# Attention, top-1 routing and two feed-forward layers on one core: the routing's row comparisons move between GpSimd, VectorE and ScalarE

## The chip, the cores and the metric

The kernel runs on one core of a Trainium2 chip. The metric is the device time of one execution in microseconds, the median of three runs. Engine names are those of the profile: PE is TensorE (PEld its weight loads), DVE is VectorE, ACT is ScalarE, POOL is GpSimd, SP is SyncE, which issues most DMAs.

## The reference, cut to what matters

```
x = attention(q, k, v)                  # 2 x 8 heads, 768 positions, window 128 and 4 sinks -> 1536 x 512
logits = x @ w_gate                     # 1536 tokens x 8 experts
for idx in argsort(-logits.flatten()):  # best (token, expert) pair first
    tok, e = idx // 8, idx % 8
    if assigned[tok] >= 0 or counts[e] >= 192: continue
    assigned[tok] = e; counts[e] += 1
for e in range(8):
    out[assigned == e] = relu(x[assigned == e] @ w1[e]) @ w2[e]     # 512 -> 1024 -> 512
g = prelu(out @ w_in, alpha)            # 512 -> 2048
return g @ w_out                        # 2048 -> 512
```

The loop over sorted pairs is a strict order of decisions, and the kernel has to give every token the same expert as that loop. It does so without a sort.

## The kernel before, in words

**Routing in stages.** Each stage closes one expert, the one that fills up first. Every living token has a best logit `m` among the experts still open and a one-hot row `oh` that names the expert. For a token t the kernel counts, per expert, how many living tokens have a better best logit (ties by index). The tokens whose count is below 192 for the expert that closes get it; its column is then struck out and the next stage begins. There are seven such stages (s = 0 to 6); the eighth expert takes what is left. Stages 0 and 1 work on 12 blocks of 128 tokens, stages 2 and 3 on 9, stages 4 to 6 on 6, because the living tokens are packed together between them by an indirect DMA each (`compact`).

**The counts.** `mrow` (128 x 1536, fp32) holds all best logits as one row, the same in each of the 128 partitions. For a block c1 of 128 tokens, whose own logits are a column `m[:, c1]`, the kernel makes a bf16 0/1 matrix `cm` (128 x 1536) of "row value is below own value", and PE multiplies it with `oh` of the block, 128 columns at a time (`count`, line 1042), and adds up over the blocks. A row of `cm` has three parts: the columns left of the block's own 128 (strictly below), the diagonal 128 columns (with the tie rule, through the constant triangle `tri`) and the columns to the right (below or equal).

There are two ways to make a block's `cm`:

- The direct way: one DVE `scalar_tensor_tensor` for the diagonal (line 991, `diag`) and one DVE `tensor_scalar` that compares fp32 to bf16 for each side (line 995, `side`).
- The way by differences (`via`): first the difference own minus row in bf16 (`minus`), in two instructions that together cover the row, on ACT (line 1000) or on POOL (line 1002), whichever the planner finds free first; then DVE compares the bf16 differences with zero (line 1010 for the sides, line 1006 for the diagonal).

Which blocks go by differences is set by `VIA`: in stage s those with `c1 * 7 % 12 < VIA[s]`. With VIA = (12, 6, 4, 2, 0, 0, 0) these are all blocks in stage 0, blocks 0, 2, 4, 7, 9, 11 in stage 1, 0, 2, 7 in stage 2, 0 and 7 in stage 3, and none later.

**Stage 0 in two groups.** Attention ends with the last token blocks. Stage 0 therefore starts on blocks 0 to 8 (columns 0 to 1151, group 0) while attention is still at blocks 9 to 11, and goes on with those (group 1) when their gate logits are there. In group 1 the old nine blocks get only the 384 new columns, by a direct comparison each (line 995), and the new three blocks get the whole row. The chain into group 1 is: transposes of x (PE, line 590), their high and low halves (ACT line 593, DVE line 595), gate (PE, line 619), logits (ACT, line 625), best logit (DVE, line 948), broadcast to `mrow` (PE line 976, ACT line 980).

After each stage the expert's tokens are named (`ohs`, line 1139, PE lines 1251 or 1273), their rows of x are gathered by an indirect DMA that POOL issues (line 1292), transposed on PE (line 1305), and the expert's two products follow (lines 1387 to 1394; experts 0 and 1 in plain fp32, line 1394, with their relu on ACT at line 1426). After two experts each, one chunk of 384 tokens runs through the last two layers (lines 1462 and 1483). Weights and activations of the later products are split into a high and a low half: the high half by ACT (line 1339), the low half by POOL or DVE (`lows`, line 1330). Line 807 is a step of unpacking w_in and w_out on POOL or DVE.

**What sets the order.** Each engine runs its instructions in the order in which a planner (`Plan.run`) emitted them. The planner is a list scheduler with an estimated time per task and engine. A task that names several engines goes to the first of them unless another would finish more than `bias` earlier (0.85 us by default; `EVEN` = 0.0 for the differences). So another estimate changes not only where a task goes, but the order of everything behind it. `cm` is a ring of 3 buffers (11 in stage 0): a buffer is written anew when PE has done the counts of its last user.

Of the kernel before, what the change touches and what calls it, by code (L numbers as in the profile page):

```python
# [211 lines left out]
AF = mybir.ActivationFunctionType  # L212
OP = mybir.AluOpType
# [24 lines left out]
def dve(n):  # L238
    return n / 960 + 0.065
# [491 lines left out]
def act_sb(n):  # L731
    return n / 1200 + 0.093
# [106 lines left out]
class Routed:  # L839
# [9 lines left out]
    BY_ROW = 2  # L849
    BY_DMA = (2, 3, 4, 5, 6)  # L850
    PLAIN, PLAIN2 = (0, 1), (0, 1)
    VIA = (12, 6, 4, 2, 0, 0, 0)

    def __init__(self, tc, nc, plan, ctx, logits, l_blocks, cd, md, xd, x_blocks, ident):
        self.tc, self.nc, self.plan, self.xd, self.x_blocks = tc, nc, plan, xd, x_blocks
# [71 lines left out]
    def closing(self, s, st, groups, r_bank, hold=(), fetched=False):  # L927

        nc, task, seq, ident, mrow, tri = self.nc, self.plan.task, self.seq, self.ident, self.mrow, self.tri  # L930
# [12 lines left out]
        for a, b in groups:  # L943
            n = b - a
# [11 lines left out]
            if fetched:  # L956
# [4 lines left out]
                     r=[m.part(a)], w=[ps], after=hold)  # L961
# [23 lines left out]
            for a1, b1 in done:  # L985
                for c1 in range(a1, b1):
                    cm, cut = self.r_cm.new(), []
                    at = c1 * 128

                    def diag(c1=c1, cm=cm, at=at):  # L990
                        nc.vector.scalar_tensor_tensor(cm.tile[:, at:at + 128], mrow[:, at:at + 128], m.tile[:, c1:c1 + 1],  # L991
                                                       tri, OP.subtract, OP.is_lt)

                    def side(x, y, op, c1=c1, cm=cm):
                        nc.vector.tensor_scalar(cm.tile[:, x:y], mrow[:, x:y], m.tile[:, c1:c1 + 1], None, op)  # L995

                    def minus(e, x, y, c1=c1, cm=cm):
                        to, rows_, own = cm.tile[:, x:y], mrow[:, x:y], m.tile[:, c1:c1 + 1]
                        if e == "ACT":
                            nc.scalar.activation(to, rows_, AF.Identity, scale=-1.0, bias=own)  # L1000
                        else:
                            nc.gpsimd.tensor_scalar(to, rows_, -1.0, own, OP.mult, OP.add)

                    def diag_d(cm=cm, at=at):
                        d = cm.tile[:, at:at + 128]
                        nc.vector.tensor_tensor(d, d, self.trih, OP.is_gt)

                    def side_d(x, y, op, cm=cm):
                        d = cm.tile[:, x:y]
                        nc.vector.tensor_scalar(d, d, 0.0, None, OP.is_gt if op is OP.is_lt else OP.is_ge)  # L1010

                    lo = 0 if a1 == a else a
                    via = a1 == a and (c1 * 7 % 12) < self.VIA[s]
                    rr = [m.part(a1), *(rows if a1 == a else fresh)]
                    if a1 == a:
                        sides = ((0, at, at + 128, None), (1, 0, at, OP.is_lt), (2, at + 128, b * 128, OP.is_le))
                    else:
                        sides = ((2, a * 128, b * 128, OP.is_le),)
                    if via:
                        for x, y, kk in ((0, at + 128, (0, 1)), (at + 128, b * 128, (2,))):  # L1020
                            if y > x:
                                n = y - x
                                seq.append(task({"ACT": act_sb(n), "POOL": n * 1.0e-3 + 0.02},
                                                lambda e, x=x, y=y, f=minus: f(e, x, y), r=rr, bias=self.EVEN,
                                                w=[cm.part(k) for k in kk if k != 1 or at]))
                    for k, x, y, op in sides:
                        if y == x:
                            continue
                        if op is None:
                            us, fn = (0.135, diag_d) if via else (0.265, diag)  # L1030
                        elif via:
                            us, fn = dve((y - x) / 4), lambda x=x, y=y, op=op, f=side_d: f(x, y, op)
                        else:
                            us, fn = dve((y - x) / 2) + 0.065, lambda x=x, y=y, op=op, f=side: f(x, y, op)
                        cut.append(cm.part(k))
                        seq.append(task({"DVE": us}, fn, r=() if via else rr, w=cut[-1:]))
                    counted.append(cnt.part(len(counted)))

                    def count(c1=c1, cm=cm, lo=lo, b=b):
                        begun.append(c1)  # L1040
                        for c in range(lo, b):
                            nc.tensor.matmul(v()[:, c], lhsT=cm.tile[:, c * 128:(c + 1) * 128], rhs=oh.tile[:, c1],  # L1042
                                             start=(len(begun) == 1 and c == lo),
                                             stop=(len(begun) == len(counted) and c == b - 1), skip_group_check=True)

                    task({"PE": 0.026 * (b - lo)}, count, r=[oh.part(a1), *cut], w=counted[-1:],
                         after=hold)
# [564 lines left out]
```

## Time and profile before

| what | value |
|---|---|
| time, median of 3 runs (lowest, highest) | 680.67 us (679.73, 681.04) |
| the profiled execution: its own time | 686.22 us |
| its span, first to last instruction | 684.5 us |
| PE, PEld busy | 598.6 us, 511.1 us |
| DVE, POOL, ACT busy | 486.9 us, 405.4 us, 393.0 us |

The stretches that the text speaks of, in microseconds from the start of the span: attention 0 to 117, stage 0 from 104 to 131 (group 0 to 118, group 1 from 118), stage 1 from 133 to 170 beside expert 0 (PE 146 to 178), the gather of expert 1's tokens to 184, expert 1 to 213, stages 2 and 3 from 208 to 305 beside the first chunk, stages 4, 5 and 6 around 390, 415 and 495 to 525. A busy time includes the time in which an instruction, already begun, is held up. A row of the timeline gives start, duration, engine, line, operation, tiles and shapes, the number of merged instructions, and in brackets the idle time before it with what ended it.

### The profile page before, as it was taken

To read this page: it belongs to the slowest core of one execution; us is meant where nothing else is said; L and a number is where in the kernel's file an instruction comes from. 1 tells how busy PE (TensorE), PEld (TensorE's weight loads), DVE (VectorE), ACT (ScalarE), POOL (GpSimd) and SP (SyncE) were. 2 spreads that over 40 slices of the span, in tenths; PEclk is the share of its full clock that TensorE was granted. 3 is DMA by queue.
4 is the path that set the end of the run, shared out by engine and by line. 5 is a ranking of instruction groups with operands and counts; after the bars stand their busy time and mean duration, and the time that the engine had idled before them with its cause. 6 is when DMAs were issued, how large, how long until landed. Compare 5 with 4: busy or idle time off the path is not lost.

```text
span 684.5 us, 12142 instructions
## 1 busy us (share of the span) xinstructions
PE 598.6 (87%) x4248; PEld 511.1 (75%) x4249; DVE 486.9 (71%) x1165; ACT 393.0 (57%) x835; POOL 405.4 (59%) x445
## 2 busy tenths in 40 slices
PE   5699996688688878789999989998998999899996
PEld 3467775467587766668889868697997888889994
DVE  4779998879656989882897587578766556874330
ACT  5668886364355755434776434377653447665552
POOL 4657735254734657446777655676675657766663
PEclk9589997569899889899999999999999999999999
DMA  7856343326877426003650021256000326500001
GB/s 208 257 109 141 94 94 109 124 95 233 284 264 236 124 62 220 24 0 107 218 155 5 24 93 47 93 173 209 28 1 0 116 63 197 190 30 1 0 1 46
DMA packets 41221, 76.57 MB, mean 112 GB/s; under 512 B 16324, under 2 KB 23016, under 8 KB 41064
## 3 DMA queue, kind: packets, MB, share of 16 engines
q1 hardware_dynamic: 38376, 68.87, 33.2%
q0 software_dynamic: 2784, 6.93, 3.0%
q8 instruction: 33, 0.54, 0.3%
q14 instruction: 28, 0.23, 0.1%
HBM read 66.75 MB, written 6.42 MB: 107 GB/s over the span
## 4 chain that ended last, share of the span: by engine, by line
PE 33%; DVE 11%; ACT 4%; DMA 3%; issue 2%; POOL 1%; POOLq 0%; ACTq 0%; DVEq 0%
PE o L1483 13%; PE h L1462 13%; PE h L1387 4%; DVE h L1379 3%; ACT spl L1339 2%; DVE spl L1330 2%; PE h L1389 2%; DVE cm L995 2%; DVE jt L1375 1%; DMA xg<-xd,sidx 1%; DMA raw<-w 1%; PE r L1305 1%; DVE x L1330 1%; DVE cm L991 1%; ACT jt L1374 1%
## 5 line engine op out<-in xcount | busy, mean ns | idle before, releaser
L1330 POOL TENSOR_TENSOR spl<-w,spl 128x512 fp32r<-128x512 f32 x107 | 143.7, 1345 | 91.0 <-ACT spl L1339 85.6
L1483 PE MATMUL o<-spl,gt 128*128 128x512 f32 x576 | 155.5, 414 | 4.7 <-DVE gt L1330 2.8
L1462 PE MATMUL h<-x,spl 128*128 128x384 f32 x768 | 150.3, 345 | 1.2 <-DVE x L1330 0.9
L1462 PEld LDWEIGHTS h<-x,spl 128*128 128x128 f32 x768 | 138.2, 193 | 7.7 <-DVE x L1330 2.6
L1483 PEld LDWEIGHTS o<-spl,gt 128*128 128x128 f32 x576 | 109.2, 196 | 26.7 <-DVE gt L1330 3.3
L1339 ACT CAST spl<-w 128x512 fp32r<-128x512 f32 x126 | 77.5, 616 | 30.7 <-PE o L1483 25.9
L1330 POOL TENSOR_TENSOR spl<-raw,spl 128x512 fp32r<-128x512 f32 x53 | 71.6, 1355 | 36.1 <-ACT spl L1339 26.1
L1466 ACT ACTIVATE t<-h,slope 128x384 f32<-128x384 f32 x64 | 37.1, 580 | 76.2 <-PE h L1462 76.2
L1468 DVE SCALAR_TENSOR_TENSOR v<-h,way,t 128x384 f32<-128x384 f32 x64 | 39.2, 613 | 55.7 <-ACT t L1466 55.7
L1339 ACT CAST spl<-raw 128x512 fp32r<-128x512 f32 x93 | 56.1, 620 | 19.6 <-PE o L1483 11.9
L1387 PE MATMUL h<-xT,spl 128*128 128x384 f32 x192 | 56.7, 363 | 9.4 <-DVE jt L1375 9.4
L1330 DVE TENSOR_TENSOR spl<-raw,spl 128x512 fp32r<-128x512 f32 x43 | 42.7, 994 | 25.5 <-ACT spl L1339 25.2
L1387 PE MATMUL h<-h,spl 128*128 128x384 f32 x192 | 55.9, 360 | 1.6 <-DVE jt L1375 1.4
L1470 ACT CAST gt<-v 128x384 fp32r<-128x384 f32 x64 | 32.9, 513 | 35.8 <-DVE v L1468 34.3
L1330 DVE TENSOR_TENSOR gt<-v,gt 128x384 fp32r<-128x384 f32 x39 | 38.2, 981 | 20.3 <-ACT gt L1470 20.3
L480 ACT ACTIVATE P<-sm,mn 128x260 f32<-128x260 f32 (+1 forms) x96 | 43.3, 490 | 10.4 <-DVE mn L469 9.6
L1389 PE MATMUL h<-xT,spl 128*128 128x192 f32 x192 | 48.0, 250 | 0.0
L1389 PE MATMUL h<-h,spl 128*128 128x192 f32 x192 | 48.0, 250 | 0.0
L1042 PEld LDWEIGHTS <-cm 128*128 128x128 bf16 x558 | 20.5, 100 | 35.0 <-DVE cm L995 24.4
L995 DVE TENSOR_SCALAR cm<-mrow,m 128x384 bf16<-128x384 f32 (+8 forms) x75 | 44.0, 624 | 1.1 <-ACT mrow L980 1.1
L1387 PEld LDWEIGHTS h<-xT,spl 128*128 128x128 f32 x192 | 36.0, 188 | 11.4 <-DVE jt L1375 11.2
L469 DVE CUSTOM_DVE_ANT_0 sm<-s,mask 128x260 f32<-128x260 f32 (+1 forms) x96 | 35.3, 398 | 10.9 <-PE s L459 10.8
(223 smaller groups left out, 1271.6 us busy)
## 6 DMA issues: line engine op xcount, KB each, us to landing
raw<-w SPq DMA_DIRECT2D x64, 512.0 KB, 3.9
r<-w_in SPq DMA_DIRECT2D x16, 512.0 KB, 4.2
r<-w_out SPq DMA_DIRECT2D x16, 512.0 KB, 4.7
vraw<-v SPq DMA_DIRECT2D x4, 768.0 KB, 10.4
xd<-x SPq DMA_DIRECT2D x12, 256.0 KB, 2.2
k<-kT SPq DMA_DIRECT2D x11, 260.0 KB, 5.6
q<-qT SPq DMA_DIRECT2D x11, 256.0 KB, 2.7
mrow<-md SPq DMA_DIRECT2D x2, 576.0 KB, 5.3
```

Source lines behind the costliest of these rows:

```text
L469: task({"DVE": dve(n)}, lambda: nc.vector.tensor_tensor_reduce(out=sm.tile[:, :n], in0=s.tile[:, :n], in1=mask[:, :n], scale=-0.125, scala ...
L480: task({"ACT": act(n) + 0.137}, lambda h=h, sm=sm, mn=mn: nc.scalar.activation(P[t].tile[:, h, :n], sm.tile[:, :n], AF.Exp, bias=mn.tile, ...
L995: nc.vector.tensor_scalar(cm.tile[:, x:y], mrow[:, x:y], m.tile[:, c1:c1 + 1], None, op)
L1330: eng.tensor_tensor(*aps(), OP.subtract)
L1339: (nc.scalar.copy if e == "ACT" else nc.vector.tensor_copy)(b.tile[:, 0], get())
L1387: nc.tensor.matmul(ps.tile[:, 0:2 * CAP], lhsT=w[:, 0, k], rhs=x.rearrange("p a t -> p (a t)"), start=first and k == 0, stop=False, skip_g ...
L1389: nc.tensor.matmul(ps.tile[:, CAP:2 * CAP], lhsT=w[:, 1, k], rhs=x[:, 0], start=False, stop=last and k == len(xs) - 1, skip_group_check=True)
L1462: nc.tensor.matmul(ps.tile[:, 0:CH], lhsT=w[:, i, k], rhs=x[:, j], start=(k == n == 0), stop=(k == KD - 1 and n == 2))
L1466: task({"ACT": act(CH)}, lambda: nc.scalar.activation(t.tile, ps.tile[:, 0:CH], AF.Copy, scale=slope), r=[ps, weights.way_res], w=[t])
L1468: task({"DVE": dve(CH) + 0.065}, lambda: nc.vector.scalar_tensor_tensor(v.tile, ps.tile[:, 0:CH], way, t.tile, OP.mult, OP.max), r=[ps, t, ...
L1470: task({"ACT": act_sb(CH)}, lambda: nc.scalar.copy(gt.tile[:, 0], v.tile), r=[v], w=[gt.part(0)])
L1483: nc.tensor.matmul(ops[t].tile, lhsT=gt.tile[:, i, sl], rhs=wo.tile[:, j], start=(f == n == 0), stop=(f == FB - 1 and n == 2))
```

## The change: what it does

```diff
-    VIA = (12, 6, 4, 2, 0, 0, 0)
+    VIA = (8, 6, 4, 2, 0, 0, 0)
+    SHORT = 768
...
-                    def side(x, y, op, c1=c1, cm=cm):
-                        nc.vector.tensor_scalar(cm.tile[:, x:y], mrow[:, x:y], m.tile[:, c1:c1 + 1], None, op)
-
-                    def minus(e, x, y, c1=c1, cm=cm):
-                        to, rows_, own = cm.tile[:, x:y], mrow[:, x:y], m.tile[:, c1:c1 + 1]
-                        if e == "ACT":
-                            nc.scalar.activation(to, rows_, AF.Identity, scale=-1.0, bias=own)
-                        else:
-                            nc.gpsimd.tensor_scalar(to, rows_, -1.0, own, OP.mult, OP.add)
+                    def side(e, x, y, op, c1=c1, cm=cm):
+                        (nc.gpsimd if e == "POOL" else nc.vector).tensor_scalar(cm.tile[:, x:y], mrow[:, x:y], m.tile[:, c1:c1 + 1], None, op)
+
+                    def minus(x, y, c1=c1, cm=cm):
+                        nc.scalar.activation(cm.tile[:, x:y], mrow[:, x:y], AF.Identity, scale=-1.0, bias=m.tile[:, c1:c1 + 1])
...
-                                seq.append(task({"ACT": act_sb(n), "POOL": n * 1.0e-3 + 0.02},
-                                                lambda e, x=x, y=y, f=minus: f(e, x, y), r=rr, bias=self.EVEN,
+                                seq.append(task({"ACT": act_sb(n) + 0.1}, lambda x=x, y=y, f=minus: f(x, y), r=rr,
                                                 w=[cm.part(k) for k in kk if k != 1 or at]))
...
+                        us = {}
                         if op is None:
-                            us, fn = (0.135, diag_d) if via else (0.265, diag)
+                            us["DVE"], fn = (0.135, diag_d) if via else (0.265, diag)
                         elif via:
-                            us, fn = dve((y - x) / 4), lambda x=x, y=y, op=op, f=side_d: f(x, y, op)
+                            us["DVE"], fn = dve((y - x) / 4), lambda x=x, y=y, op=op, f=side_d: f(x, y, op)
                         else:
-                            us, fn = dve((y - x) / 2) + 0.065, lambda x=x, y=y, op=op, f=side: f(x, y, op)
+                            us["DVE"], fn = dve((y - x) / 2) + 0.165, lambda e, x=x, y=y, op=op, f=side: f(e, x, y, op)
+                            if y - x <= self.SHORT or not s:
+                                us["POOL"] = (y - x) * 1.1e-3 + 0.15
                         cut.append(cm.part(k))
-                        seq.append(task({"DVE": us}, fn, r=() if via else rr, w=cut[-1:]))
+                        seq.append(task(us, fn, r=() if via else rr, w=cut[-1:], bias=self.EVEN if s == 0 else None))
```

Differences are formed by ACT alone; POOL forms none. The comparison of a side (line 995) may run on POOL as well as on DVE: in stage 0 for any width and wherever the planner expects the earlier end, in later stages for sides of up to 768 columns and only where POOL would end more than 0.85 us earlier. In stage 0 only the blocks with `c1 * 7 % 12 < 8` go by differences, which leaves blocks 3, 5 and 8 of group 0 and block 10 of group 1 to the direct way. The planner's estimate for a difference on ACT and for a direct comparison on DVE rises by 0.1 us each. What is computed stays the same.

## Rows read from the trace of the kernel before

**Rows 1.** The page: the line of the span and the busy times with their shares and instructions.

```profile
span 684.5 us, 12142 instructions
PE 598.6 (87%) x4248; PEld 511.1 (75%) x4249; DVE 486.9 (71%) x1165; ACT 393.0 (57%) x835; POOL 405.4 (59%) x445
```

**Rows 2.** Busy times by stretch: the stretch, its length, then busy time and instructions of PE, PEld, DVE, ACT and POOL, the granted clock of TensorE, the DMA share and GB/s. Group 0 and group 1 of stage 0, stage 1, the gather of expert 1, stages 2 and 3.

```profile
105.80:118.10 12.30, 7.22 (x143) 5.78 (x139) 11.63 (x37) 7.83 (x16) 8.31 (x10) 0.72 0.38 129
119.80:126.30 6.50, 3.11 (x51) 2.23 (x51) 6.31 (x17) 4.29 (x6) 2.22 (x2) 0.50 0.01 1
135.00:162.00 27.00, 22.86 (x219) 18.90 (x218) 22.37 (x48) 15.04 (x25) 13.61 (x11) 0.74 0.40 136
162.00:186.00 24.00, 17.38 (x124) 14.88 (x122) 18.87 (x53) 9.66 (x19) 14.76 (x20) 0.94 0.87 303
213.00:305.00 92.00, 76.20 (x459) 62.32 (x458) 83.16 (x158) 49.32 (x90) 53.94 (x43) 0.85 0.33 104
```

**Rows 3.** The waits of PE: whom it waited for, microseconds in total, times, longest. The first line is of the whole span; the others are what falls into 128 to 162, 215 to 262, 262 to 305, 385 to 402 and 490 to 526.

```profile
PE r L1042 <- DVE cm L995: 15.7, 17, 2.9
...
PE r L1042 <- DVE cm L995: 3.9, 4, 2.7
...
PE r L1042 <- DVE cm L995: 2.5, 3, 2.0
...
PE r L1042 <- DVE cm L995: 4.6, 4, 2.9
...
PE r L1042 <- DVE cm L995: 2.4, 3, 1.3
...
PE r L1042 <- DVE cm L995: 2.3, 3, 1.6
```

**Rows 4.** The timeline of group 0 of stage 0 and of the gate that opens group 1, on DVE, ACT and POOL.

```profile
106.79 7.83 POOL L1002 TENSOR_SCALAR cm<-mrow,m 128x896 bf16<-128x896 f32 x9 [0.44 <-ACT mrow L980]
112.35 1.05 DVE L1006 TENSOR_TENSOR cm<-cm,trih 128x128 bf16<-128x128 bf16 x1
112.79 0.69 ACT L593 ACTIVATE xT<-pt,scv 128x512 f16<-128x512 f32 x1 [0.25 <-PE pt L590]
113.33 1.46 DVE L1010 TENSOR_SCALAR cm<-cm 128x384 bf16<-128x384 bf16 x2
115.62 0.74 DVE L595 SCALAR_TENSOR_TENSOR xT<-pt,scv,xT 128x512 f16<-128x512 f32 x1
116.88 0.27 ACT L625 ACTIVATE L<-pv,scv 128x8 f32<-128x8 f32 x1 [3.12 <-PE pv L619]
116.99 0.21 DVE L1006 TENSOR_TENSOR cm<-cm,trih 128x128 bf16<-128x128 bf16 x1
117.53 0.21 DVE L1006 TENSOR_TENSOR cm<-cm,trih 128x128 bf16<-128x128 bf16 x1
118.00 0.16 DVE L948 TENSOR_REDUCE m<-L 128x3 f32<-128x24 f32 x1
```

**Rows 5.** The timeline of group 1 of stage 0, on POOL and DVE; the row at 120.22 holds two of the nine comparisons of the row at 119.89.

```profile
119.95 2.22 POOL L1002 TENSOR_SCALAR cm<-mrow,m 128x256 bf16<-128x256 f32 x2 [5.33 <-ACT mrow L980]
119.89 4.46 DVE L995 TENSOR_SCALAR cm<-mrow,m 128x384 bf16<-128x384 f32 x9 [1.09 <-ACT mrow L980]
120.22 2.16 DVE L995 TENSOR_SCALAR cm<-mrow,m 128x384 bf16<-128x384 f32 x2
122.30 0.40 DVE L995 TENSOR_SCALAR cm<-mrow,m 128x384 bf16<-128x384 f32 x1
124.27 0.21 DVE L1006 TENSOR_TENSOR cm<-cm,trih 128x128 bf16<-128x128 bf16 x1
125.69 0.51 DVE L1010 TENSOR_SCALAR cm<-cm 128x1408 bf16<-128x1408 bf16 x1
```

**Rows 6.** Single prices: the first three lines are of the timeline on POOL and DVE; the others are groups of instructions by shape, with busy time and the mean of one in ns.

```profile
138.58 0.38 POOL L1002 TENSOR_SCALAR cm<-mrow,m 128x128 bf16<-128x128 f32 x1
138.94 1.43 POOL L1002 TENSOR_SCALAR cm<-mrow,m 128x1408 bf16<-128x1408 f32 x1
...
395.03 0.34 DVE L991 SCALAR_TENSOR_TENSOR cm<-mrow,m,tri 128x128 bf16<-128x128 f32 x1
...
L1330 POOL TENSOR_TENSOR gt<-v,gt 128x384 fp32r<-128x384 f32 x25 | 28.0, 1120 | 20.6 <-ACT gt L1470 20.6
...
L995 DVE TENSOR_SCALAR cm<-mrow,m 128x1280 bf16<-128x1280 f32 x2 | 1.7, 873 | 0.0
...
L1000 ACT ACTIVATE cm<-mrow,m 128x1024 bf16<-128x1024 f32 x5 | 5.6, 1144 | 0.0
L1000 ACT ACTIVATE cm<-mrow,m 128x128 bf16<-128x128 f32 x5 | 2.0, 401 | 1.2 <-DMA mrow<-md 1.2
```

**Rows 7.** The timeline of stage 1 and of the gather behind it, on DVE, POOL and PE.

```profile
138.99 2.58 DVE L1006 TENSOR_TENSOR cm<-cm,trih 128x128 bf16<-128x128 bf16 x1 [1.47 <-POOL cm L1002]
140.34 1.15 POOL L807 TENSOR_TENSOR w<-w,sg 128x512 f32<-128x512 f32 x1
143.16 2.44 POOL L1002 TENSOR_SCALAR cm<-mrow,m 128x896 bf16<-128x896 f32 x1 [1.67 <-PE r L1042]
181.29 0.24 PE L1305 MATMUL r<-ident,xg 64*128 64x64 f32 x1 [3.00 <-DMA xg<-xd,sidx]
183.91 2.58 PE L1305 MATMUL r<-ident,xg 128*128 128x128 f32 x7 [2.38 <-DMA xg<-xd,sidx]
```

## The prediction, made before the changed kernel ran

> **What bounds the kernel now.** I read the busy times first [rows 1]: PE is busy for 598.6 of 684.5 us and the change touches none of its products, so what it can move is PE's idle time and whatever feeds PE. The stretches come second [rows 2]: PE works 7.2 of 12.3 us in group 0 and 3.1 of 6.5 us in group 1 of stage 0, at a granted clock of 0.72 and 0.50, while DVE is busy for 11.63 and 6.31 us of the same stretches. Routing there is a serial piece ahead of everything else, and DVE sets its length. Later PE is fuller and waits in places; its waits [rows 3] put 15.7 us down to DVE's direct comparisons (line 995): 3.9 us in stage 1, 2.5 and 4.6 us in stages 2 and 3, 2.4 us in stage 4, 2.3 us in stage 6. The timelines come last, because they show why DVE is slow there. In group 0 POOL forms nine differences without a break, 7.83 us, and in that time a DVE instruction of 0.21 us takes 1.05 us and two that follow take 1.46 us [rows 4]. In group 1 two comparisons take 2.16 us, beside POOL's 2.22 us, where one takes 0.40 us once POOL is done [rows 5]. In stage 1 one of 0.21 us takes 2.58 us and ends as POOL falls idle [rows 7]. So POOL and DVE hold each other up on these instructions, and the reader should see "DVE busy" there as partly waiting.
>
> **Stage 0, group 0.** Before, POOL has ten differences (6,272 columns, 8.31 us busy [rows 2]) and ACT seven (4,096 columns), counted one by one in the two timelines; together they are nine rows of 1,152. After, six blocks remain on ACT alone: 6,912 columns in 12 instructions. A difference costs 0.295 us plus 0.83 ns a column (from 1,144 ns for 1,024 and 401 ns for 128 [rows 6]); consecutive ones overlap by about 0.1 us, which is my estimate from the gap between their sum and ACT's busy time. That adds 2,816 x 0.83 ns = 2.3 us and five instructions of 0.2 us, 3.3 us in all, to an ACT that is idle for 12.30 - 7.83 = 4.5 us of this stretch [rows 2]. It fits, with 1.2 us to spare.
> On DVE an unhindered block by differences takes 0.54 us (116.99 to 117.53 [rows 4]); nine would take 4.9 us. Blocks 3, 5 and 8 now need a diagonal each (0.34 us as recorded [rows 6], 0.27 us less the 0.07 us by which such rows overlap: 0.40 us recorded, 0.33 us from start to start [rows 5]) and five sides (384, 640, 640, 384, 1,024 columns) that mostly go to an idle POOL. No row shows a comparison on POOL. From below I price it as POOL's difference, 0.27 us plus 0.82 ns a column (0.38 us for 128, 1.43 us for 1,408 [rows 6]), so 0.59 us for 384; from above as POOL's subtraction of two inputs, 1.12 us for 384 [rows 6]. I take the lower, because both are one-input instructions of the same shape on the same tiles. The five sides are then 3.9 us instead of 8.3 us of POOL, ending near 111 rather than 114.6, and DVE is free of POOL when the last gate comes.
> What that gives on the path: the low half for the gate (line 595) starts at 115.62 though its high half was ready at 113.48 (112.79 + 0.69), 2.1 us late, and the best logit (line 948) at 118.00 though the logits were ready at 117.15, 0.85 us late [rows 4]. Both go away at best: 3.0 us. ACT, now nearly full, may put one difference of up to 1.14 us ahead of line 593 and again ahead of line 625. So between -3.0 and -0.7 us; if ACT's queue runs over, up to +1.2 us. I take -1.4 us.
>
> **Stage 0, group 1.** Nine 384-column comparisons cost 0.33 us each from start to start when nothing holds them (122.30 to 124.27 for six [rows 5]), and POOL will take about four, since it is planned at 0.57 us (384 x 1.1 ns + 0.15) and DVE at 0.43 us, so that POOL ends earlier whenever DVE has one in hand. Block 10 goes direct: diagonal 0.27 us, 0.80 us for 1,280 columns (873 ns recorded [rows 6], less the overlap) and 0.19 us for 128. Blocks 9 and 11 keep 0.64 us each (124.27 to 124.91, and 0.65 us to 126.20). If POOL and DVE exclude each other the sum is 4 x 0.59 + 5 x 0.33 + 1.26 + 1.29 = 6.6 us against 6.31 us now; if they ran side by side it would be 4.2 us; if POOL also gets the 1,280 columns, 7.1 us; at the upper price 8.7 us. The rows show holding up, so I take +0.3 us, between -2.1 and +2.4. Stage 0 together: -1.1 us.
> [...]
> [...]
>
> **Stage 1.** POOL's five differences, one of them 2.44 us long for 896 columns [rows 7], move to ACT, which is busy for 15.04 of 27 us [rows 2]. With them goes most of the 2.37 us that DVE lost at 138.99, the rest of which is line 807's 1.15 us [rows 7], and the PE wait of 2.7 us behind it [rows 3]. PE's counts stand between expert 0's products, so a faster `cm` brings them forward only where the planner puts them forward. What the end of stage 1 sets is the gather of expert 1: PE waits 3.00 and 2.38 us for it [rows 7], 5.4 us, the most that can be had. Against it: the same five, 3,712 columns, cost ACT 3,712 x 0.83 ns + 5 x 0.295 us = 4.6 us, ahead of the relu of expert 0. Between -5.4 and +1.5 us; I take -1.5 us.
>
> **Stages 2 to 6.** Few differences leave POOL here: four in stages 2 and 3 by its timeline, none later. Sides of up to 768 columns may go to POOL where DVE is over 0.85 us behind. The four waits after 213 add up to 11.8 us [rows 3], the outer end of a gain. But POOL also makes the low halves that PE waits for, and every compare there holds DVE's diagonal. Between -4 and +2 us; I take -0.6 us.
>
> Sum: -1.4 + 0.3 - 1.5 - 0.6 = -3.2 us. The profiled execution took 686.22 us (span 684.5 us and 1.7 us around it), 5.55 us over the median of 680.67 us; a difference of this kind carries over as it is: 683.0 us for such an execution, 677.5 us for the median.
>
> **Rivals.**
> (1) The compares share out but the time doesn't fall. DVE and POOL take turns, the planner gives POOL little beyond stage 0 because of its bias (then the change does less than it says), and ACT's fuller queue eats what group 0 gains: 680.4 us. For it: the held-up rows. Against it: POOL's turns in group 0 halve in any case.
> (2) Slower: ACT becomes the bound. All differences pass through one queue. If the last one of group 0 ends after 117.2, where the logits are ready now, group 1 starts later by up to one wide difference, 1.14 us; in stage 1 two differences of 1,280 or 1,536 columns (about 1.4 us each) ahead of a relu leave PE without a free bank, since there are three. 1.1 + 2 x 1.4 - 0.9 (what DVE still gains) = +3.0 us: 683.7 us. For it: 1.2 us of slack. Against it: ACT is idle for 12 of 27 us in stage 1.
> (3) Slower: a compare on POOL costs like its two-input work, 1.12 us for 384 columns. Group 1 grows by 2.4 us and group 0 gains nothing (3,072 columns keep POOL as long as now), stage 1 gains half: 2.4 - 0.75 = +1.7 us, 682.4 us.
> (4) Much faster: stage 1 ends 4 us earlier so that the gather's wait nearly goes, and half of the 11.8 us of later waits melts through POOL: -1.1 - 4 - 3 = -8 us, 672.5 us.
>
> **How the numbers follow.** Forecast 0.50 (own range 674 to 679.5), (1) 0.21, (2) 0.13, (3) 0.06, (4) 0.10. About 0.2%, 1.4 us, is what a measurement tells from no change: faster takes the forecast without its edge, 0.47, and (4), 0.57; same takes (1) and that edge, 0.24; slower takes (2) and (3), 0.19. The range, 671 to 684 us, takes in the other cases except the far half of (4) and of (2), and covers that any new estimate reorders all instructions behind it.
>
> **What would show it.** Right: in group 0 DVE rows of line 1006 fall to 0.21 us after about 111; line 948 starts near 116.5 instead of 118.00; in group 1 POOL holds about four 384-column compares near 0.6 us, and DVE rows beside them stretch; the wait for expert 1's gather is below 5.4 us. Wrong: POOL's compare of 384 columns near 1 us; ACT without gaps up to line 625; PE waits for `cm` from POOL; or line 995 nearly all on DVE after stage 0.

## The result, and the profile after

The changed kernel took 687.88 us (median of 4 runs, 686.28 to 688.18), the kernel before beside it 680.86 us (679.73 to 681.93): ratio 1.0111 [1.0074, 1.0148], slower by 7.0 us. The forecast was 677.5 us, range 671 to 684: the sign was wrong and the time lies outside the range. The profiled execution of the changed kernel took 687.92 us. The profiled execution of the kernel before was a slow one: up to its first best logits, which start at 104.20 us and in the other traces at 99 to 102, its granted clock was 0.89 against 1.00 in the changed kernel, and behind them the two differ by 0.03 at most, so stages are compared below from that instruction on.

The page of the changed kernel, span and busy times, beside [rows 1]:

```profile
span 686.2 us, 12140 instructions
PE 599.8 (87%) x4248; PEld 513.6 (75%) x4249; DVE 484.6 (71%) x1150; ACT 401.1 (58%) x849; POOL 420.1 (61%) x439
```

PE's work is the same to 1.2 us. POOL is busy for 14.7 us more, with six instructions fewer. Most of that is the exchange itself: its 21 differences took 21.0 us before, its 19 comparisons take 34.0 us now.

The waits of PE over the whole span (whom for, microseconds in total, times, longest), beside the first of [rows 3]:

```profile
PE r L1041 <- DVE cm L996: 15.7, 11, 6.0
PE s L1041 <- POOL cm L996: 7.4, 5, 3.0
PE r L1041 <- POOL cm L996: 3.7, 2, 2.2
```

Line 996 is now the comparison of a side (995 before), 999 ACT's difference, 1041 the count. 11.1 us of waits for POOL's comparisons are new: 7.4 us in stage 0 (tile `s`), 3.7 us in stage 1 (`r`). The wait for DVE's comparisons has the same sum as before, 15.7 us, but not in the same places. In stage 1 the 3.9 us of before are gone; behind stage 1 the wait has grown from 11.8 us [rows 3] to the whole 15.7 us. What falls into 214 to 305, 385 to 440 and 490 to 540 (stages 2 and 3, 4, 6):

```profile
PE r L1041 <- DVE cm L996: 11.8, 5, 6.0
...
PE r L1041 <- DVE cm L996: 2.4, 3, 1.3
...
PE r L1041 <- DVE cm L996: 1.5, 3, 0.8
```

Stretches of the changed kernel, columns as in [rows 2]: group 0, group 1, stage 1.

```profile
101.60:111.20 9.60, 6.30 (x135) 5.43 (x131) 8.88 (x29) 9.29 (x19) 7.81 (x4) 0.69 0.42 140
112.60:122.40 9.80, 2.52 (x58) 2.04 (x59) 5.99 (x15) 4.93 (x7) 8.79 (x5) 0.50 0.00 1
131.00:162.00 31.00, 24.72 (x226) 20.98 (x225) 22.25 (x47) 18.89 (x31) 17.18 (x11) 0.75 0.42 142
```

In group 1 the engine that sets the length has changed: DVE was busy for 6.31 of 6.5 us, now it is idle for 3.8 of 9.8 us and POOL is busy for 8.79 of them, with five instructions.

**Group 0** (timeline on POOL, ACT and DVE, beside [rows 4]):

```profile
101.69 7.81 POOL L996 TENSOR_SCALAR cm<-mrow,m 128x384 bf16<-128x384 f32 x4 [2.85 <-ACT mrow L981]
108.10 0.72 ACT L593 ACTIVATE xT<-pt,scv 128x512 f16<-128x512 f32 x1
108.67 0.98 DVE L1007 TENSOR_SCALAR cm<-cm 128x512 bf16<-128x512 bf16 x1
109.57 0.73 DVE L595 SCALAR_TENSOR_TENSOR xT<-pt,scv,xT 128x512 f16<-128x512 f32 x1
110.83 0.27 ACT L625 ACTIVATE L<-pv,scv 128x8 f32<-128x8 f32 x1 [0.31 <-PE pv L619]
111.13 0.18 DVE L949 TENSOR_REDUCE m<-L 128x3 f32<-128x24 f32 x1
```

Four comparisons (2,432 columns) keep POOL for 7.81 us, nearly as long as nine differences did. They end at 109.50, just ahead of the last gate. The low half (line 595) starts 0.75 us after its high half (108.10 + 0.72) instead of 2.1 us: a DVE comparison of 512 columns ahead of it takes 0.98 us beside POOL, where the same shape takes 0.28 us at 110.22. The best logit starts 0.03 us after the logits (110.83 + 0.27) instead of 0.85 us.

**Group 1** (timeline on POOL, DVE and PE, beside [rows 5]):

```profile
113.27 8.79 POOL L996 TENSOR_SCALAR cm<-mrow,m 128x128 bf16<-128x128 f32 x5 [3.77 <-DVE cm L1007]
113.29 3.10 DVE L996 TENSOR_SCALAR cm<-mrow,m 128x384 bf16<-128x384 f32 x6
117.84 0.84 DVE L1007 TENSOR_SCALAR cm<-cm 128x1408 bf16<-128x1408 bf16 x1
122.12 0.80 PE L1041 MATMUL s<-oh,cm 128*128 128x8 bf16 x24 [3.04 <-POOL cm L996]
122.96 0.26 DVE L1053 SCALAR_TENSOR_TENSOR both<-s,far 128x96 f32<-128x96 f32 x1 [4.28 <-PE s L1041]
```

DVE has all its parts done at 118.68 (117.84 + 0.84) and then stands idle for 4.28 us, PE for 3.04 us, until POOL's last comparison ends at 122.06 (113.27 + 8.79). The prices of these comparisons, by shape (busy time, mean of one in ns, idle time before):

```profile
L996 POOL TENSOR_SCALAR cm<-mrow,m 128x384 bf16<-128x384 f32 x9 | 12.9, 1443 | 9.0 <-PE r L1041 6.2 <-ACT mrow L981 2.8
...
L996 DVE TENSOR_SCALAR cm<-mrow,m 128x384 bf16<-128x384 f32 x14 | 8.9, 664 | 0.1
...
L996 POOL TENSOR_SCALAR cm<-mrow,m 128x1280 bf16<-128x1280 f32 x1 | 3.8, 3780 | 0.0
```

1,443 ns for 384 columns where I took 590 and had 1,120 as the bound from above, and 3.78 us for 1,280, which the planner expects to last 1.56 us (1,280 x 1.1 ns + 0.15).

**Stage 1** (timeline on POOL, PE, ACT and DVE, beside [rows 7]; the last four rows are the ranks that end the stage and PE's last product of expert 0 and its waits for expert 1's gather):

```profile
142.03 2.00 POOL L996 TENSOR_SCALAR cm<-mrow,m 128x384 bf16<-128x384 f32 x1 [3.21 <-PE r L1041]
147.48 6.17 POOL L996 TENSOR_SCALAR cm<-mrow,m 128x768 bf16<-128x768 f32 x3 [3.45 <-PE r L1041]
150.62 0.33 PE L1041 MATMUL r<-oh,cm 128*128 128x8 bf16 x7 [1.52 <-POOL cm L996]
153.12 0.30 PE L1041 MATMUL r<-oh,cm 128*128 128x8 bf16 x5 [2.18 <-POOL cm L996]
153.59 1.76 ACT L999 ACTIVATE cm<-mrow,m 128x1024 bf16<-128x1024 f32 x2 [4.14 <-PE r L1041]
154.78 0.23 DVE L1003 TENSOR_TENSOR cm<-cm,trih 128x128 bf16<-128x128 bf16 x1 [2.26 <-ACT cm L999]
169.66 0.25 DVE L1082 TENSOR_REDUCE rk<-rf 128x12 f32<-128x96 f32 x1
173.52 7.12 PE L1393 MATMUL h<-h,raw 128*128 128x192 f32 x32
181.28 0.24 PE L1304 MATMUL r<-ident,xg 64*128 64x64 f32 x1 [0.64 <-DMA xg<-xd,sidx]
184.04 2.57 PE L1304 MATMUL r<-ident,xg 128*128 128x128 f32 x7 [2.51 <-DMA xg<-xd,sidx]
```

This is a chain that closes on itself. PE waits for POOL's comparison with the products of expert 0 queued behind the count; the ring has three `cm` buffers, so ACT's next difference waits 4.14 us for PE's counts, as POOL itself had waited 3.45 us for them; DVE then waits 2.26 us for ACT.

The table gives each part's length in microseconds, from single instructions of each trace: group 0 from the first best logits (line 948, or 949) to the second, group 1 from there to the ranks of stage 0 (line 1083, or 1082), stage 1 from those ranks to its own; "chunk 0" and "end" count from the first best logits to the end of the first chunk's products and of the span; "rest" lies between these two. The last two columns are medians and the ratio to before, each beside runs of before on the same chip; medians of different chips don't compare (before itself has 679.81, 683.24 and 683.47 us on three of them).

| kernel | group 0 | group 1 | stage 1 | chunk 0 | end | rest | median | ratio |
|---|---|---|---|---|---|---|---|---|
| before | 13.8 | 12.3 | 39.1 | 218.6 | 580.3 | 361.7 | | |
| after | 11.1 | 15.3 | 43.3 | 224.0 | 586.2 | 362.1 | 687.88 | 1.0111 [1.0074, 1.0148] |
| e1 no comparison on POOL | 11.5 | 11.4 | 37.0 | 214.3 | 578.4 | 364.2 | 679.50 | 0.9946 [0.9916, 0.9976] |
| e2 planner's price x 2.8 | 11.2 | 12.0 | 37.3 | 211.8 | 578.3 | 366.5 | 678.25 | 0.9923 [0.9897, 0.9949] |
| e3 POOL in stage 0 only | 11.1 | 15.3 | 36.7 | 216.3 | 580.8 | 364.4 | 683.47 | 1.0009 [0.9985, 1.0033] |
| e4 POOL in later stages only | 11.5 | 11.4 | 41.7 | 219.8 | 584.3 | 364.5 | 684.13 | 1.0007 [0.9974, 1.0041] |
| e5 before, differences on ACT only | 13.1 | 14.1 | 36.4 | 212.5 | 577.7 | 365.2 | 679.54 | 0.9994 [0.9959, 1.0028] |
| e7 before, VIA 8 only | 13.6 | 13.0 | 39.0 | 215.4 | 575.9 | 360.5 | 679.26 | 1.0008 [0.9965, 1.0052] |
| e8 e1 with the old estimates | 12.6 | 11.4 | 38.2 | 212.1 | 574.8 | 362.7 | 676.64 | 0.9953 [0.9920, 0.9985] |
| e9 no 1,280 columns on POOL | 11.1 | 12.7 | 41.3 | 219.2 | 581.8 | 362.5 | 686.65 | 1.0042 [1.0009, 1.0074] |
| e10 measured price | 11.8 | 11.6 | 38.0 | 218.2 | 578.7 | 360.4 | 680.64 | 0.9940 [0.9909, 0.9970] |

### The profile page after: what moved, and what is told of

Same layout as the page of the kernel before. It is cut to its first block, busy times and chain, and to the rows that moved or that the text cites. A ratio compares the mean times of both kernels' runs of the same rounds, so it can differ in the third digit from the quotient of the medians.

```text
span 686.2 us, 12140 instructions
## 1 busy us (share of the span) xinstructions
PE 599.8 (87%) x4248; PEld 513.6 (75%) x4249; DVE 484.6 (71%) x1150; ACT 401.1 (58%) x849; POOL 420.1 (61%) x439
## 4 chain that ended last, share of the span: by engine, by line
PE 34%; DVE 10%; DMA 4%; ACT 3%; issue 3%; POOL 1%; POOLq 0%; DVEq 0%; SPq 0%; ACTq 0%
PE o L1482 13%; PE h L1461 12%; PE h L1386 5%; DMA raw<-w 3%; PE h L1388 2%; ACT spl L1338 2%; DVE spl L1329 2%; DVE cm L996 2%; DVE h L1378 1%; DVE x L1329 1%; PE r L1304 1%; DVE cm L992 1%; DVE jt L1374 1%; POOL spl L1329 1%; DMA xg<-xd,sidx 1%
## 5 line engine op out<-in xcount | busy, mean ns | idle before, releaser
L1329 POOL TENSOR_TENSOR spl<-w,spl 128x512 fp32r<-128x512 f32 x110 | 148.3, 1350 | 86.0 <-ACT spl L1338 79.1
L1482 PE MATMUL o<-spl,gt 128*128 128x512 f32 x576 | 153.5, 408 | 1.6 <-ACT gt L1469 0.8
L1482 PEld LDWEIGHTS o<-spl,gt 128*128 128x128 f32 x576 | 106.6, 193 | 22.6 <-issue 1.5
L1329 POOL TENSOR_TENSOR spl<-raw,spl 128x512 fp32r<-128x512 f32 x52 | 70.0, 1350 | 38.6 <-ACT spl L1338 29.1
L1386 PE MATMUL h<-xT,spl 128*128 128x384 f32 x192 | 58.5, 370 | 8.1 <-DVE jt L1374 8.1
L1329 DVE TENSOR_TENSOR gt<-v,gt 128x384 fp32r<-128x384 f32 x40 | 37.3, 933 | 18.5 <-ACT gt L1469 18.5
L996 POOL TENSOR_SCALAR cm<-mrow,m 128x384 bf16<-128x384 f32 (+6 forms) x19 | 33.8, 1788 | 17.7 <-PE r L1041 11.1
L1329 POOL TENSOR_TENSOR gt<-v,gt 128x384 fp32r<-128x384 f32 x24 | 30.4, 1269 | 18.7 <-ACT gt L1469 18.6
```

The source lines that it names most:

```text
L996: (nc.gpsimd if e == "POOL" else nc.vector).tensor_scalar(cm.tile[:, x:y], mrow[:, x:y], m.tile[:, c1:c1 + 1], None, op)
L1329: eng.tensor_tensor(*aps(), OP.subtract)
L1386: nc.tensor.matmul(ps.tile[:, 0:2 * CAP], lhsT=w[:, 0, k], rhs=x.rearrange("p a t -> p (a t)"), start=first and k == 0, stop=False, skip_g ...
L1482: nc.tensor.matmul(ops[t].tile, lhsT=gt.tile[:, i, sl], rhs=wo.tile[:, j], start=(f == n == 0), stop=(f == FB - 1 and n == 2))
```

## The experiments

Four theories stood against each other. A: a comparison costs POOL some 3 ns a column, which neither the planner nor I reckoned with. B: ScalarE, alone with the differences, is the new bound (the second rival). C: it is the reordering by new estimates and a new VIA, whatever the engines. D: POOL's comparison is quick by itself and was only held up by VectorE.

**e1: no comparison on POOL.** Edit of the changed kernel:

```diff
-                            if y - x <= self.SHORT or not s:
+                            if False:
```

> The changed kernel with every direct comparison on VectorE; differences stay on ScalarE alone and 8 of 12 blocks of stage 0 go by differences. Theory A (a comparison on GpSimd takes about 3 ns a column, planned as 1.1): group 1 of stage 0 loses the 4.3 us in which VectorE idles for the last comparison of GpSimd, stage 1 loses PE's 3.7 us wait for GpSimd, and what group 0 gained (2.7 us) stays: 677 to 680 us. Theory B (ScalarE alone with the differences is the cost): 685 us or more. Theory C (the loss comes of the new order of everything, tied to no part): anywhere from 680 to 690 us, with group 1 no shorter than 15 us between the second head and the ranks.

Measured: 679.50 us, ratio 0.9946 [0.9916, 0.9976]. Everything else of the change is still there, and the loss has turned into a gain. Group 1 is back at 11.4 us, stage 1 at 37.0. In group 1 DVE alone makes nine comparisons of 384 columns in the time in which it made six beside POOL (timeline on DVE; then the ranks of stage 1 and the gather's waits as above):

```profile
114.52 3.06 DVE L996 TENSOR_SCALAR cm<-mrow,m 128x384 bf16<-128x384 f32 x9 [0.41 <-ACT mrow L981]
161.16 0.25 DVE L1082 TENSOR_REDUCE rk<-rf 128x12 f32<-128x96 f32 x1
175.45 0.34 PE L1304 MATMUL r<-ident,xg 64*128 64x64 f32 x1 [4.70 <-DMA xg<-xd,sidx]
176.82 2.58 PE L1304 MATMUL r<-ident,xg 128*128 128x128 f32 x7 [1.03 <-DMA xg<-xd,sidx]
```

B falls here: ScalarE has the same differences as in the changed kernel.

**e2: the planner told a higher price.** POOL stays allowed, at 3.05 ns a column:

```diff
-                                us["POOL"] = (y - x) * 1.1e-3 + 0.15
+                                us["POOL"] = (y - x) * 3.05e-3 + 0.1
```

> The changed kernel with the planner told what a comparison on GpSimd took in the trace after the change: 3.05 ns a column and 0.1 us, instead of 1.1 ns and 0.15 us. Theory A: the planner gives GpSimd a few narrow sides only where it is idle for long, the 1,280 columns of group 1 go to VectorE, 677 to 681 us. Theory B: 685 us or more, since ScalarE's part is unchanged. Theory C: 680 to 690 us.

Measured: 678.25 us, 0.9923 [0.9897, 0.9949]. The same permission with another number in the estimate is worth 1.9%. The planner now gives POOL eight comparisons instead of nineteen, the widest of 768 columns. So the fault lies in the price that the planner was told, through the number and width of what it sends to POOL, and not in the permission.

**e3 and e4: POOL's comparisons in stage 0 only, and in the later stages only.**

```diff
-                            if y - x <= self.SHORT or not s:
+                            if not s:
```

> The changed kernel with comparisons on GpSimd in stage 0 alone. Theory A: stage 0 stays as in the changed kernel (26.4 us from the first head to the ranks), stage 1 falls from 43.2 us to 39 us or less: 683 to 685 us. Theory B: 686 to 688 us, no change. Theory C: no rule.

```diff
-                            if y - x <= self.SHORT or not s:
+                            if y - x <= self.SHORT and s:
```

> The changed kernel with comparisons on GpSimd in stages 1 to 6 alone. Theory A: group 1 of stage 0 is 3 us shorter than in the changed kernel, stage 1 stays near 43 us: 682 to 685 us. With the run that has them in stage 0 alone the two parts add up to the loss of 7 us against the run without any. Theory B: 686 to 688 us. Theory C: no rule.

Measured, on the same chip as e1 and e2: 683.47 and 684.13 us, 4.0 and 4.6 us over e1, neither to be told from before (1.0009, 1.0007). The parts move alone: e3 has group 1 of the changed kernel (15.3 us) and the stage 1 of e1 (36.7), e4 the opposite (11.4 and 41.7). In the traces e3 and e4 end 2.3 and 5.8 us later than e1, together 8.1, the changed kernel 7.7 us, so there the two losses add up. By the medians the two make 8.6 us, while the changed kernel's ratio stands 1.65% over e1's, some 11 us that are known to about 3 us: whether there is a third loss is not shown.

**e5: before, with the differences on ACT alone.** VIA stays 12 in stage 0:

```diff
-                                seq.append(task({"ACT": act_sb(n), "POOL": n * 1.0e-3 + 0.02},
-                                                lambda e, x=x, y=y, f=minus: f(e, x, y), r=rr, bias=self.EVEN,
+                                seq.append(task({"ACT": act_sb(n) + 0.1},
+                                                lambda x=x, y=y, f=minus: f("ACT", x, y), r=rr,
```

> The kernel before, with all differences on ScalarE (planned 0.1 us dearer each) and nothing else changed: all 12 blocks of stage 0 still go by differences and VectorE does all comparisons. Theory A (only GpSimd's comparisons cost time): stage 0 has nine rows of 1,152 columns on ScalarE, 10,368 x 0.83 ns + 18 x 0.2 us = 12.2 us and some 2.7 us of other work against 12.3 us of group 0 now, so stage 0 grows by 2 to 3 us; stage 1 loses GpSimd's differences and falls from 39.1 to 37 us as in the run without comparisons on GpSimd; 680 to 683 us. Theory B (ScalarE alone is the cost): 686 us or more.

Measured: 679.54 us, 0.9994 [0.9959, 1.0028]. Even with all twelve blocks of stage 0 on ACT the kernel isn't slower. Stage 0 is longer by 1.2 us (27.3 us against 26.1) where I expected 2 to 3, stage 1 shorter (36.4 against 39.1): what the second rival said of ACT holds in stage 0 and fails in stage 1.

**e6: the prices by themselves.** At the end of the changed kernel POOL runs a row of instructions alone, of 384 and 1,280 columns; at the very end, POOL and DVE run side by side. Its own time is not that of the kernel.

```
for n in (384, 1280):
    mult + add | is_lt | is_le | is_lt constant | min | subtract | subtract, is_lt     # lines 1568 to 1574
is_lt to fp32 | is_lt from bf16 | tensor_tensor subtract, 384 columns                  # lines 1575 to 1577
```

> The changed kernel with a row of instructions behind its end, on data that no longer matter, so that its time is not to be compared: GpSimd's difference (two arithmetic operations), comparisons with a column and with a constant, a minimum, a subtraction, a subtraction with a comparison behind it, all on 384 and 1,280 columns with nothing else running, and then eight comparisons of VectorE beside one comparison of GpSimd, and beside one difference. Theory A: a comparison takes about 1.25 us for 384 columns and 3.7 us for 1,280 even alone, a difference 0.6 and 1.3 us. If instead GpSimd was only held up by VectorE in the changed kernel (theory D), the comparison alone takes about as long as the difference. [...]

Timeline on POOL (384 columns: mult + add, is_lt, min, subtract, then the subtraction of two inputs):

```profile
677.81 0.59 POOL L1568 TENSOR_SCALAR cm<-mrow,dead 128x384 bf16<-128x384 f32 x1
678.50 1.24 POOL L1569 TENSOR_SCALAR cm<-mrow,dead 128x384 bf16<-128x384 f32 x1
...
682.45 1.26 POOL L1572 TENSOR_SCALAR cm<-mrow,dead 128x384 bf16<-128x384 f32 x1
683.79 1.26 POOL L1573 TENSOR_SCALAR cm<-mrow,dead 128x384 bf16<-128x384 f32 x1
...
713.29 1.00 POOL L1577 TENSOR_TENSOR cm<-mrow 128x384 f32<-128x384 f32 x1
```

By shape, 1,280 columns (subtract then is_lt, is_lt, subtract, mult + add):

```profile
L1574 POOL TENSOR_SCALAR cm<-mrow,dead 128x1280 bf16<-128x1280 f32 x1 | 4.6, 4605 | 0.1
...
L1569 POOL TENSOR_SCALAR cm<-mrow,dead 128x1280 bf16<-128x1280 f32 x1 | 3.5, 3525 | 0.1
L1573 POOL TENSOR_SCALAR cm<-mrow,dead 128x1280 bf16<-128x1280 f32 x1 | 3.5, 3525 | 0.1
...
L1568 POOL TENSOR_SCALAR cm<-mrow,dead 128x1280 bf16<-128x1280 f32 x1 | 1.3, 1335 | 0.1
```

With DVE idle a comparison of 384 columns takes 1.24 us, one of 1,280 takes 3.53 us: 2.55 ns a column and 0.26 us ((3.525 - 1.242) / 896). D falls; A stands, at 2.55 ns instead of some 3. Mult + add has 0.83 ns a column by the same two widths.

**e7 and e8: the reordering.** e7 is before with the new VIA alone:

```diff
-    VIA = (12, 6, 4, 2, 0, 0, 0)
+    VIA = (8, 6, 4, 2, 0, 0, 0)
```

> The kernel before with 8 instead of 12 blocks of stage 0 by differences, still shared between ScalarE and GpSimd, and all comparisons on VectorE. Theory A: group 0 has fewer differences on GpSimd, group 1 loses one of two on GpSimd; stage 0 falls from 26.1 us to about 24 us, stage 1 stays near 39 us; 678 to 680 us. If ScalarE alone is worth something by itself in stage 0, the run without comparisons on GpSimd (22.9 us) stays ahead of this one.

e8 is e1 with the estimates of before for ACT's difference and DVE's comparison:

```diff
-                                seq.append(task({"ACT": act_sb(n) + 0.1}, lambda x=x, y=y, f=minus: f(x, y), r=rr,
+                                seq.append(task({"ACT": act_sb(n)}, lambda x=x, y=y, f=minus: f(x, y), r=rr,
...
-                            us["DVE"], fn = dve((y - x) / 2) + 0.165, lambda e, x=x, y=y, op=op, f=side: f(e, x, y, op)
+                            us["DVE"], fn = dve((y - x) / 2) + 0.065, lambda e, x=x, y=y, op=op, f=side: f(e, x, y, op)
```

> The changed kernel without comparisons on GpSimd and with the planner's old estimates: no 0.1 us added to a difference on ScalarE nor to a direct comparison on VectorE. Theory A: no difference clear of noise from the run that keeps the new estimates, 676 to 681 us; stage 0 within 0.5 us of 22.9 us. Theory C (order is what counts): off by more than 3 us either way.

Measured: 679.26 us, 1.0008 [0.9965, 1.0052], and 676.64 us, 0.9953 [0.9920, 0.9985]. e7's stage 0 (26.5 us) missed my 24 us, its stage 1 (39.0) met the 39: with POOL still making the differences, VIA alone gives nothing that can be told from before. e8 keeps e1's gain, so C falls as the cause of the loss. The estimates aren't free of effect, though: group 0 is 12.6 us with the old ones and 11.5 with the new, and e8's stage 0 (24.0 us) missed the 22.9 us that I expected by more than my 0.5.

**e9: only the 1,280 columns off POOL.** Edit of the changed kernel:

```diff
-                            if y - x <= self.SHORT or not s:
+                            if y - x <= (1024 if not s else self.SHORT):
```

> The changed kernel with one limit moved: in stage 0, too, sides over 1,024 columns may not go to GpSimd. That leaves only the 1,280 columns of block 10 for VectorE; the planner still believes in its 1.1 ns a column for all other sides. If group 1 ends late because of that one comparison (3.5 to 3.8 us on GpSimd, nothing behind it but the counts), group 1, 15.3 us in the changed kernel, falls by 2 to 3.5 us, to 12 to 13.3 us, and stage 1 stays near 43 us, since nothing of it changes: 684.5 to 686.5 us. If instead GpSimd's four or five comparisons of 384 columns would have held group 1 up by themselves, it stays at 14.5 us or more and the time within 1 us of the changed kernel's.

Measured: 686.65 us, 1.0042 [1.0009, 1.0074], still slower than before. Group 1 falls from 15.3 to 12.7 us, inside what was expected of the single wide comparison; stage 1 stays long, at 41.3 us. Timeline on POOL, DVE and PE:

```profile
112.78 5.66 POOL L996 TENSOR_SCALAR cm<-mrow,m 128x128 bf16<-128x128 f32 x4 [3.77 <-DVE cm L1007]
117.21 0.87 DVE L996 TENSOR_SCALAR cm<-mrow,m 128x1280 bf16<-128x1280 f32 x1
118.50 1.36 PE L1041 MATMUL s<-oh,cm 128*128 128x8 bf16 x45 [1.78 <-POOL cm L996]
```

DVE makes in 0.87 us what POOL needs 3.78 us for. Even so PE's last wait, 1.78 us, is still for POOL, whose fourth comparison ends at 118.44. One instruction had 2.6 us of group 1's 3.9 us over e1, the smaller ones the rest.

**e10: the measured price, with the old estimates.** e8 with POOL allowed again:

```diff
-                            if False:
-                                us["POOL"] = (y - x) * 1.1e-3 + 0.15
+                            if y - x <= self.SHORT or not s:
+                                us["POOL"] = (y - x) * 2.55e-3 + 0.26
```

> The change with GpSimd planned at the price measured alone, 2.55 ns a column + 0.26 us, and without the two rises of 0.1 us in the estimates of ScalarE's difference and VectorE's comparison. If only the price was wrong with the change, this is as fast as the two versions without GpSimd comparisons or with the higher price (676.6 to 679.5 us): stage 0 at 23 to 24 us, stage 1 at 36.5 to 38.5 us, 676 to 679 us, ratio 0.992 to 0.997. [...]

Measured: 680.64 us, 0.9940 [0.9909, 0.9970]. The planner now gives POOL ten comparisons instead of nineteen, none of 1,280 columns, and the gain is that of e1, e2 and e8, whose intervals overlap (0.9923 to 0.9953). The time itself lies 1.6 us over the 676 to 679 us that I had expected if only the price was wrong, but before takes 683.24 us on this chip, so the ratio counts, and it lies inside the 0.992 to 0.997 expected for that case. All four beat both kernels; which of them is best, and whether a few comparisons on POOL help at all, these runs can't tell.

## Why the prediction was wrong

By the traces, before to after: group 0 -2.7 us (forecast -1.4), group 1 +3.0 (+0.3), stage 1 +4.1 (-1.5), all behind it +1.5 (-0.6); together +5.9 (-3.2).

**The step that failed is the price of a comparison on POOL**; that stage 1 has such comparisons at all, which the sum put at nothing, is the second. I priced it from below "as POOL's difference", 0.59 us for 384 columns, and "from above as POOL's subtraction of two inputs, 1.12 us", and took the lower "because both are one-input instructions of the same shape on the same tiles". Shape and number of inputs did not set it: e6 has 1.24 us alone against 0.59 us for the difference of the same shape, and in place the comparison took 1.44 us in the mean. Its price lies above both bounds, since the row for the upper one was not dear enough: subtracting two inputs takes 1.00 us alone where a comparison with one takes 1.24. What the trace offered was two prices of two operations, and neither was the operation in question.

**Group 1.** The planner's choice was nearly foreseen (about four comparisons of 384 columns, "if POOL also gets the 1,280 columns, 7.1 us"): POOL got three of 384, one of 128 and the 1,280. These five instructions alone last 8.79 us, where the whole stretch was 6.5 us before and 8.7 us was my sum of both engines in turns at the upper price. The +3.0 us lie beyond even the upper end that I gave, +2.4: that end had four comparisons at 1.12 us and the 1,280 columns on DVE.

**Stage 1.** A gain like "most of the 2.37 us that DVE lost" did come once POOL was out of the way: e1, e3 and e5, with the differences on ACT, have 36.4 to 37.0 us against 39.1, a gain of 2.1 to 2.7 where I had 1.5. The changed kernel shows a loss because POOL's four comparisons there (2.00 us for one and 6.17 us for three) hold up counts that stand in PE's queue ahead of expert 0's products; e4 minus e1 puts 4.7 us on them, e3 against the changed kernel 6.5 us. In the sum I had weighed POOL's comparisons only in stage 0 and in "Stages 2 to 6", and none in stage 1, although the planner's rule for sides up to 768 columns holds there.

**Group 0** was right in kind and better in size: the two late starts shrank from 3.0 us together to 0.8 us, though POOL's comparisons lasted 7.81 us and not 3.9 us. That they ended only 0.7 us after the last gate's high half was ready is luck. And about 1.1 us of the gain hangs on the new estimates (12.6 us in e8 against 11.5 in e1), which the forecast had not priced.

**Stages 2 to 6** lost instead of gaining: the wait for DVE's comparisons there is 15.7 us against 11.8. POOL's comparisons aren't the cause, since e1 has 14.9 us there without any. In stages 2 and 3 alone it is 7.1 us before, 11.8 after, 11.3 in e1, 6.6 in e8 with the old estimates, but 4.7 in e2 with the new ones: what sets it stays open. Nor does "every compare there" hold DVE's diagonal: beside POOL's two comparisons from 216.38 to 219.98 two diagonals (line 992, at 217.60 and 219.33) take 0.34 us each, as long as the unhindered one of [rows 6].

**The rivals.** The third, slower because a comparison on POOL is dear, had the mechanism and the sign, at 0.06; its 682.4 us was short because it took 1.12 us for 384 columns, left the 1,280 columns on DVE and let stage 1 still gain, while it gave group 0 no gain at all. The second (ACT) falls by e1. What I forecast is nearly what the change does without POOL's comparisons: 677.5 to 680.67 is 0.9953, e1 measured 0.9946. That is luck in part: in e1's trace group 0, group 1 and stage 1 give -2.3, -0.9 and -2.1 us, and the rest takes 3.5 us back, where the sum had -1.4, +0.3, -1.5 and -0.6.

**The signs to look for.** Three that were to show the forecast right came true in a kernel that is slower. "DVE rows of line 1006 fall to 0.21 us": they take 0.21 to 0.23 us after 110. "line 948 starts near 116.5", which is 12.3 us after the first best logits: it starts 11.1 us after them. And "the wait for expert 1's gather is below 5.4 us": the gather's wait is 3.15 us (0.64 + 2.51). It fell because PE came to it late, at 180.64 (173.52 + 7.12). In e1, which is faster, the same wait is 5.73 us (4.70 + 1.03). The smaller wait for the transfer was here no sign of a faster kernel. Two of those listed under wrong told the truth: "POOL's compare of 384 columns near 1 us" and "PE waits for `cm` from POOL". A third came as well and did no harm: ACT was busy for 9.29 of 9.60 us in group 0, which was shorter all the same.

**POOL and DVE side by side.** In group 1 six comparisons on DVE took 3.10 us beside POOL and nine took 3.06 us without. In e6 a copy of 128 columns on DVE that starts 0.06 us after POOL's comparison (timeline on POOL and DVE) lasts as long as it:

```profile
714.26 3.52 POOL L1581 TENSOR_SCALAR cm<-mrow,dead 128x1280 bf16<-128x1280 f32 x1
...
714.32 3.54 DVE L1578 CAST cm<-cm 128x128 bf16<-128x128 f32 x1 [45.27 <-POOL cm L1577]
...
717.90 3.60 DVE L1580 TENSOR_SCALAR cm<-mrow,dead 128x384 bf16<-128x384 f32 x8
...
721.93 1.38 POOL L1586 TENSOR_SCALAR cm<-mrow,dead 128x1280 bf16<-128x1280 f32 x1
...
721.97 0.23 DVE L1583 CAST cm<-cm 128x128 bf16<-128x128 f32 x1 [0.47 <-POOL cm L1582]
722.23 4.48 DVE L1585 TENSOR_SCALAR cm<-mrow,dead 128x384 bf16<-128x384 f32 x8
```

In the first pair DVE's eight comparisons start only at 717.90, 0.12 us after POOL's comparison ends at 717.78 (714.26 + 3.52), and take 3.60 us with POOL idle. In the second, beside a difference on POOL, a copy of the same shape starts 0.04 us after POOL and takes 0.23 us all the same, while the eight comparisons behind it take 4.48 us instead of 3.60. Why that copy went free is not shown. Where DVE is held, a slow comparison on POOL costs twice, by its own length (3.52 us in the first pair) and by what it keeps DVE from (3.3 us there, 3.54 instead of 0.23).

**What stays open.** e1 is 4.3 us ahead of before at the end of the first chunk and 1.9 us at the end; e2 is 6.8 and 2.0 us ahead. Part of an early gain is given back later, between single traces whose "rest" differs by up to 6 us. What takes it back was not tried. Nor was the price of a comparison on POOL measured alone at widths other than the two of e6.

## What to carry to other kernels

An operation that the trace did not show had no bound from its neighbours here: the nearest rows, 0.59 and 1.12 us for 384 columns, were half and nine tenths of the price of 1.24 us. When a change lets a planner move work by an estimate, the estimate is the change; ask for each place where the rule holds what happens if it is three times too low, starting with the widest piece and with the one that is last in its stage. And judge a forecast by the time, since a wait that shrinks may only mean that the waiting engine came late (3.15 us for the gather here, 5.73 us in the faster e1).

## What the runs showed of the hardware

In e6 it is not comparing that is slow on POOL: `min` and a plain subtraction take 1.26 us for 384 columns and 3.53 us for 1,280, `is_lt` and `is_le` 1.24 to 1.25 and 3.53 us; a constant in place of the column (1.17 and 3.45 us), fp32 out (1.25 us) or bf16 in (1.24 us) changes little. The pair mult + add does twice the arithmetic in 0.59 and 1.34 us, and it isn't the pair as such, since subtract + is_lt takes 1.58 and 4.61 us. So of the forms of `tensor_scalar` tried on this engine only that one is fast, by a factor of three in the slope (0.83 against 2.55 ns a column), and it was the only one that the trace of before showed on POOL (0.70 to 0.78 us for 512 columns at lines 419, 421 and 603). The difference that POOL had been making was thus the cheapest of the forms tried, which the row of a difference alone, [rows 6], could not tell.
